# Output-gate loads of steps two to eight issued from GpSimd's queue instead of SyncE's

## The chip, the cores and the metric

The kernel runs on one core of one Trainium2 chip. The core has TensorE (PE), VectorE (DVE), ScalarE (ACT), GpSimd (POOL) and SyncE (SP), each with an instruction queue of its own that is worked through in order. The time is the device time of one execution in microseconds (us). Seven runs of the kernel before gave a median of 499.81 us, from 498.5 to 501.74.

## The reference

An mLSTM cell over 4 batches, 8 heads, 768 positions and a head width of 40 is followed by a feed-forward block with a leaky ReLU. Everything is float32. Cut to what matters:

```python
for t in range(S):
    m_new = max(f[t] + m, i[t]);  f_s = exp(f[t] + m - m_new);  i_s = exp(i[t] - m_new)
    C = f_s * C + i_s * outer(v[t], k[t]);   n = f_s * n + i_s * k[t]
    h = C @ q[t];   denom = max(abs(n . q[t]), 1)
    y[t] = sigmoid(o_gate[t]) * h / denom
x = y as (4*768, 8*40)
out = max(0.01 * (x @ w_in), x @ w_in) @ w_out      # 320 -> 2048 -> 320
```

The change touches only how `o_gate` comes into the on-chip memory. It is read at one place, the sigmoid in the last line of the loop.

## The kernel before, in words

**Tiling.** The 768 positions are cut into 12 chunks of 64, and a step is one chunk of two batches, so there are 24 steps, numbered 0 to 23. Steps 0 to 7, two groups of four, are "steps one to eight" of the change's title; the kernel's `s` counts from 0. A step on 128 partitions holds two batches of 64 positions and all 8 heads. A group of four steps makes 512 rows of `x`, on which the feed-forward block then runs; the first group uses plain matmuls (L863, L867, L970), later groups a form of Strassen's scheme with seven products (L919, L933, L1025).

**One step.** k and q come in (L500) and are turned on TensorE (L569, task T), copied out (L578, KC), and multiplied to scores (L610, SC). ACT makes the decay weights with eight exponentials (L551, E), DVE multiplies them into the scores (L618, P), TensorE applies them to the values (L692, PA), and the state C is read (L629, PC) and updated (L668, DC; L681/L679, CN; POOL's products L649, VU, and L656, CM). Then the denominator (L713 to L715, N), the output gate (ACT's tanh, L719, O, which reads the loaded `o_sb` tile; L726, G), the division (L731, XD), the turn of x (L740/L742, XT) and its copies (L756/L758, XC). A group's feed-forward products need the XC of its four steps. The tile `o_sb` has three buffers, so the load for step s waits until G of step s-3 has read the old one.

**Weights.** The weights arrive as 64-bit floats (L296/L301, L307, through three double buffers called raw) and are narrowed to 32 bits: one ACT instruction (L323, WA) and six DVE instructions (L341, L345, L349, L353, L355, L359, tasks WN) for each of the pieces 0 to 7 and each pair of later pieces. The first group's products (L863, task F j) need the narrowed piece j.

**What sets the order.** All work is put into a list of tasks, each with a due time, a cost per engine that may do it, and the tasks it needs. A greedy planner (class `Plan`, L19) places them one by one at the earliest time its costs allow, ties going to the earlier due time, and the instructions are then emitted in that order, engine by engine. Loads are tasks too, with SP as their engine; it also keeps one modelled wire on which all loads queue. So a changed cost or engine of one task can move every later task on every engine. Some transposes are preceded by fill matmuls whose results are not used (L559, `FILL`): seven before the turn of step 1's q and of step 1's x, nine before the turn of step 2's k, a few in step 4.

**Where the gate loads stand.** The load of an output gate is four DMA issues of 40 KB (L493), because heads and batches are interleaved over the partitions. They are planned in `plan_cell` (L763), in the loop at L771.

Of the kernel before, what the change touches and what calls it, by code (L numbers as in the profile page):

```python
# [18 lines left out]
class Plan:  # L19
# [9 lines left out]
    def add(self, name, key, ways, needs=(), takes=None, until=(), mode=None, wire=0.0):  # L29


        assert name not in self.tasks
        key += TUNE.get(name, 0.0) + (LATER.get(name[0], 0.0) if self.later else 0.0)
        self.tasks[name] = (key, ways, needs, takes, until, mode, wire)
# [105 lines left out]
def kernel(  # L140
# [26 lines left out]
    nc = tc.nc  # L167
# [7 lines left out]
    SG = 2 * PB  # L175
# [19 lines left out]
    def half(r):  # L195
        return slice(L * r, L * (r + 1))
# [170 lines left out]
    ACT, DVE, POOL, PE, SP = "ACT", "DVE", "POOL", "PE", "SP"  # L367
# [118 lines left out]
    def load(s, what, by=None):  # L486
        c, p = divmod(s, PB)
        d = st[s]
        if what == "o":
            d["o"] = wk.tile([P, H, D], F32, name="o_sb", bufs=NL)  # L490
            for r in range(2):
                for z in range(2):
                    (by or nc.sync).dma_start(  # L493
                        d["o"][half(r ^ z), ts(r, HH), :],
                        o_gate[2 * p + r, ts(z, HH), ts(c, L), :].rearrange("h p d -> p h d"),
                    )
            return
        dst, src = {"k": (d["kq"][0][:, :, :D], k), "q": (d["kq"][1][:, :, :D], q), "v": (d["va"][:, :, :D], v)}[what]
        for r in range(2):
            (by or nc.sync).dma_start(dst[half(r)], src[2 * p + r, :, ts(c, L), :].rearrange("h p d -> p h d"))  # L500
# [72 lines left out]
    def turned(s, i, copy):  # L573
        d = st[s]
        if "kqT" not in d:
            both = wk.tile([P, 2, PR, 2, P], F32, name="kqT")[:, 0].rearrange("p j r t -> p (j r t)")
            d["kqT"] = both.rearrange("p (i j r t) -> p i j r t", i=2, j=PR, r=2)
        copy(d["kqT"][:, i].rearrange("p j r t -> p j (r t)"), d.pop(("tp", i))[:])  # L578
# [118 lines left out]
    def valued(s, copy=None):  # L697
        d = st[s]
        pa = d.pop("pa")
        if copy:  # L700
            d["hn"] = wk.tile([P, H, D1], F32, name="hn")
        for r in range(2):
            to = d["hn"][:, ts(r, HH)]
            if copy:
                copy(to, pa[r][:])
            else:
                nc.vector.tensor_tensor(to, to, pa[r][:], op=ALU.add)
# [20 lines left out]
    def divide(s, by):  # L728
        d = st[s]
        x3 = d["x"][:].rearrange("p (h d) -> p h d", d=D)  # L730
        by.tensor_tensor(x3, x3, d["den"][:].unsqueeze(2).to_broadcast([P, H, D]), op=ALU.mult)  # L731
# [31 lines left out]
    def plan_cell(s):  # L763
# [7 lines left out]
        for what, old in (  # L771
            ("k", (("T", s - NL, 0), ("DC", s - NL))), ("q", (("T", s - NL, 1),)),
            ("v", (("VU", s - NL), ("PA", s - NL))), ("o", (("G", s - NL),)),
        ):
            if what == "q" and late_turn:
                continue
            ways = [(SP, 2.2 if what == "o" else 1.3, lambda what=what: load(s, what))]
            if (s, what) in ON_ACT:
                ways = [(ACT, 1.3, lambda what=what: load(s, what, nc.scalar))]
            add(("L", s, what), LOADS.get((s, what), at), ways, old, wire=1.4)  # L780
# [21 lines left out]
        for i in range(0 if late_turn else 2):  # L802
            add(("T", s, i), key[0], [(PE, 0.55, lambda i=i: turn(s, i))], [("L", s, "kq"[i]), ("SC", s - 2), ("PC", s - 2)], ("c", 1), [("KC", s, i)], mode=128)
            ways = [(ACT, 0.6, lambda i=i: turned(s, i, nc.scalar.copy))]
# [36 lines left out]
        if c > 0:  # L841
            ways = [(DVE, 0.62, lambda: valued(s))]
        else:
            ways = [(ACT, 0.8, lambda: valued(s, nc.scalar.copy)), (DVE, 0.62, lambda: valued(s, nc.vector.tensor_copy))]
# [4 lines left out]
        ways = [(POOL, 1.0, lambda: divide(s, nc.gpsimd))]  # L849
# [332 lines left out]
    for g in range(NG):  # L1182
        plan.later = g > 1
        for s in range(SG * g, SG * (g + 1)):
            plan_cell(s)
        plan.later = g > 0
        plan_first_ff() if g == 0 else plan_ff(g)
        if g == 0:
            for i in range(5):
                needs = [("IS", i - 1)] + list(done.values()) + ([("F", 0, j, h) for j in range(NP) for h in range(2)] if i > 2 else [])  # L1190
                plan.add(("IS", i), FF_1 - 20, [(DVE, 1.25, lambda i=i: in_sum(i))], needs)
                needs = [("WS", i - 1)] + list(done.values()) + ([("PT", n, m) for n in range(SG) for m in range(4)] if i > 2 else [])
                plan.add(("WS", i), FF_1 + PERIOD / 2 - 20, [(DVE, 1.55, lambda i=i: weight_sum(i))], needs)
# [36 lines left out]
```

## Time and profile before

| what | value |
|---|---|
| median of 7 runs | 499.81 us |
| the profiled execution's own time | 499.81 us |
| its span, first to last instruction | 498.0 us |
| busy: PE, DVE, ACT, POOL | 481.0, 375.7, 194.6, 90.4 us |
| granted TensorE clock, mean | 0.989 of full |
| DMA issues of the gate (L493) | 96, median 0.614 us to issue and 2.8 us from issue to landing |

The profile was taken in an execution that took 499.81 us, of which 1.81 us lie around the span. "Idle before" of an instruction is the time its engine stood idle ahead of it, with what ended it. SPq is the queue of DMA issues of SyncE. A window's PEclk is the mean TensorE clock granted in it, as a share of full speed.

### The profile page before, as it was taken

What the parts mean: (1) busy time and instruction counts of PE and PEld (TensorE: products, weight loads), DVE (VectorE), ACT (ScalarE), POOL (GpSimd) and SP (SyncE); (2) the same over time, 40 slices, a digit from 0 to 9 for tenths busy, and PEclk for the clock granted to TensorE, in tenths of its full rate; (3) what the DMA queues carried; (4) which work ended last, traced back from release to release, by engine and by line L of the source; (5) the groups of instructions that cost most, each with busy time, mean ns of one, the idle gap of its engine ahead of it and who ended that gap; (6) DMA issues with size and microseconds to landing.
All of it is one profiled execution on the core that took longest, in us unless ns stands there. A gap on an engine that the chain in (4) does not pass through costs nothing.

```text
span 498.0 us, 14150 instructions
## 1 busy us (share of the span) xinstructions
PE 481.0 (97%) x5622; PEld 406.5 (82%) x5622; DVE 375.7 (75%) x752; ACT 194.6 (39%) x583; POOL 90.4 (18%) x177
## 2 busy tenths in 40 slices
PE   7589899999999999999999999999999999999996
PEld 5457654677788899988899988899988899988996
DVE  4779599899999898887788688788788765445542
ACT  5452635533443552535532324641325630133200
POOL 2112001220140422403113303223202111000101
PEclk9889899999999999999999999999999999999999
DMA  6655777674564334554434453425343001100011
GB/s 126 146 122 111 214 222 165 176 132 93 117 152 78 84 75 113 119 108 97 88 65 121 80 112 72 86 37 142 75 94 71 3 1 28 26 2 0 1 28 26
DMA packets 119169, 44.95 MB, mean 90 GB/s; under 512 B 90624, under 2 KB 112448, under 8 KB 119104
## 3 DMA queue, kind: packets, MB, share of 16 engines
q1 hardware_dynamic: 117536, 43.50, 39.9%
q8 instruction: 44, 0.72, 0.6%
q10 hardware_dynamic: 1568, 0.56, 0.5%
q14 instruction: 21, 0.17, 0.1%
HBM read 40.01 MB, written 4.01 MB: 88 GB/s over the span
## 4 chain that ended last, share of the span: by engine, by line
PE 92%; SPq 3%; DMA 3%; issue 1%; ACT 0%; DVE 0%; ACTq 0%
PE po L1025 31%; PE phA L919 8%; PE po L970 7%; PE phC L919 7%; PE phB L919 7%; PE ph L863 6%; PE phB L933 4%; PE phD L919 3%; PE phD L933 3%; PE sc L610 3%; PE dC L668 2%; PE pa L692 2%; PE pc L629 2%; PE ph L867 2%; SPq L500 2%; PE tkq L569 1%
## 5 line engine op out<-in xcount | busy, mean ns | idle before, releaser
L1035 DVE TENSOR_TENSOR sums<-acts 128x1024 f32<-128x1024 f32 x50 | 62.2, 1263 | 17.8 <-PE po L1025 17.7
L1025 PE MATMUL po<-sums 128*128 128x160 f32 x480 | 69.3, 299 | 0.0
L1025 PEld LDWEIGHTS po<-sums 128*128 128x128 f32 x480 | 66.3, 190 | 0.2
L1032 ACT COPY s<-po 128x160 f32<-128x160 f32 x40 | 11.6, 291 | 91.2 <-PE po L1025 91.2
L1025 PE MATMUL po<-w_out,sums 128*128 128x160 f32 x320 | 47.1, 300 | 0.0
L731 POOL TENSOR_TENSOR x<-x,den 128x320 f32<-128x320 f32 x20 | 17.4, 868 | 163.2 <-DVE den L715 131.6
L1025 PE MATMUL po<-w_out,acts 128*128 128x160 f32 x320 | 45.8, 301 | 0.0
L551 ACT ACTIVATE w<-w,gT 128x64 f32<-128x64 f32 x160 | 40.2, 335 | 14.2 <-DVE w L542 10.6
L1025 PEld LDWEIGHTS po<-w_out,sums 128*128 128x128 f32 x320 | 44.4, 190 | 0.2
L1025 PEld LDWEIGHTS po<-w_out,acts 128*128 128x128 f32 x320 | 43.9, 190 | 0.5 <-issue 0.3
L945 ACT ACTIVATE acts<-phA 128x512 f32<-128x512 f32 x20 | 11.9, 596 | 71.5 <-PE phA L933 71.5
L970 PE MATMUL po<-w_out,acts 128*128 128x320 f32 x128 | 37.0, 437 | 0.0
L600 DVE STREAM_TRANSPOSE kqT<-q_all 128x512 f32<-128x512 f32 x32 | 34.8, 1102 | 0.0
L863 PE MATMUL ph<-xT,w_in 128*128 128x256 f32 (+1 forms) x96 | 31.4, 471 | 0.0
L970 PEld LDWEIGHTS po<-w_out,acts 128*128 128x128 f32 x128 | 23.4, 190 | 8.6
L649 POOL TENSOR_TENSOR vu<-va,gT 128x328 f32<-128x328 f32 x22 | 19.2, 874 | 57.2 <-DMA va<-in_v_dram 39.0
L1040 POOL TENSOR_TENSOR y<-s,s 128x160 f32<-128x160 f32 x10 | 12.3, 1226 | 89.9 <-ACT s L1032 89.9
L945 ACT ACTIVATE acts<-acts 128x512 f32<-128x512 f32 x40 | 24.6, 630 | 9.3 <-DVE acts L1095 9.3
L863 PEld LDWEIGHTS ph<-xT,w_in 128*128 128x128 f32 x96 | 17.9, 197 | 10.3 <-issue 7.8
L1095 DVE TENSOR_TENSOR acts<-sums,phD 128x512 f32<-128x512 f32 x20 | 13.6, 681 | 16.6 <-PE phC L933 16.6
L656 POOL TENSOR_TENSOR C<-C,gT 128x328 f32<-128x328 f32 x20 | 15.7, 786 | 52.6 <-DVE C L681 42.8
L758 ACT COPY xT<-xt 32x128 f32<-32x128 f32 x96 | 24.3, 253 | 0.9
(142 smaller groups left out, 1014.6 us busy)
## 6 DMA issues: line engine op xcount, KB each, us to landing
q_all<-in_q_dram SPq DMA_DIRECT2D x80, 80.0 KB, 2.3
raw<-in_moe_w_out_dram SPq DMA_DIRECT2D x8, 640.0 KB, 6.4
w<-a_dr SPq DMA_DIRECT2D x40, 128.0 KB, 3.0
q_all<-in_k_dram SPq DMA_DIRECT2D x64, 80.0 KB, 2.4
raw<-in_moe_w_in_dram SPq DMA_DIRECT2D x8, 512.0 KB, 4.7
k<-in_k_dram SPq DMA_DIRECT2D x48, 80.0 KB, 3.0
o_sb<-in_o_gate_dram SPq DMA_DIRECT2D x96, 40.0 KB, 2.8
va<-in_v_dram SPq DMA_DIRECT2D x46, 80.0 KB, 3.2
```

What stands on the lines that cost most here:

```text
L551: nc.scalar.activation(w[:, h, :], w[:, h, :] if c > 1 else st[s]["ab"][h], AF.Exp, bias=gT[:, c, 0, p, h : h + 1], scale=1.0,)
L600: nc.vector.transpose(lates[g, p][:, i, :, r, :].rearrange("p j (t x) -> p j x t", x=4), src)
L649: nc.gpsimd.tensor_tensor(d["vu"][:], d["va"][:], gT[:, c, 1, p].unsqueeze(2).to_broadcast([P, H, D1]), op=ALU.mult,)
L731: by.tensor_tensor(x3, x3, d["den"][:].unsqueeze(2).to_broadcast([P, H, D]), op=ALU.mult)
L758: nc.scalar.copy(xT[row : row + RH, KF, ts(b, P)].rearrange("p (r t) -> p r t", r=2), quarters[:RH, 1, at, :])
L863: nc.tensor.matmul(ph[:, cols], lhsT=w_full(kk, f), rhs=xTs[g][:, kk, cols], start=(kk == 0), stop=False)
L919: nc.tensor.matmul(po[g, j, bank][:, e], lhsT=a[:, 2 * j + e], rhs=x(), start=more != "add" and e == 0, stop=True, skip_group_check=True,)
L933: nc.tensor.matmul(po[g, j, bank][:, e], lhsT=w_rest(r, 2 * j + e), rhs=xTs[g][KR * r : KR * (r + 1), KF, ts(t, GH)], start=False, stop=Tr ...
L945: nc.scalar.activation(to, x, AF.Prelu, alpha=0.01)
L970: nc.tensor.matmul(po[n][:], lhsT=acts[:, FH * (f % 2) + f // 2, ts(n, P)], rhs=w_out[:, f, :], start=(f == 0), stop=(f == NF - 1),)
L1025: nc.tensor.matmul(po[g, n, bank][:], lhsT=a()[:, f, :], rhs=w()[:, f, :], start=not more and f == 0, stop=f == FH - 1, skip_group_check=True,
L1035: nc.vector.tensor_tensor(a_sums[slot], quarter(n, x), quarter(n, y), op=op)
```

## The change: what it does

For steps 1 to 7 the load of the output gate has POOL as its only engine, with a planned cost of 2.4 us in place of SP's 2.2 us, and its four DMAs are issued from GpSimd's queue. Step 0 and the steps from 8 on stay on SP. Nothing else is edited; the planner makes a new order from the new list.

```diff
             ways = [(SP, 2.2 if what == "o" else 1.3, lambda what=what: load(s, what))]
+            if what == "o" and 0 < s < 2 * SG:
+                ways = [(POOL, 2.4, lambda what=what: load(s, what, nc.gpsimd))]
             if (s, what) in ON_ACT:
                 ways = [(ACT, 1.3, lambda what=what: load(s, what, nc.scalar))]
             add(("L", s, what), LOADS.get((s, what), at), ways, old, wire=1.4)
```

`SG` is 4, so the condition holds for s from 1 to 7: 28 DMA issues in all.

## Prediction

> **What bounds the kernel now.** I read the page's busy row and its 40 slices, then the busy time by stretch, then the chain of waits and SP's and DVE's timelines of the first 60 us.
>
> ```profile
> PE 481.0 (97%) x5622; PEld 406.5 (82%) x5622; DVE 375.7 (75%) x752; ACT 194.6 (39%) x583; POOL 90.4 (18%) x177
> 0.00:20.00 20.00, 14.82 (x346) 11.15 (x346) 11.47 (x36) 10.48 (x35) 5.03 (x18) 1.00 0.62 133
> 20.00:40.00 20.00, 14.85 (x240) 10.32 (x237) 15.02 (x46) 10.46 (x36) 2.15 (x3) 0.83 0.58 124
> 40.00:60.00 20.00, 17.10 (x226) 12.39 (x224) 13.54 (x32) 8.97 (x25) 2.08 (x3) 0.91 0.67 165
> 60.00:80.00 20.00, 20.00 (x132) 10.69 (x132) 19.21 (x30) 9.08 (x25) 0.73 (x1) 1.00 0.79 197
> 140.00:180.00 40.00, 40.00 (x523) 34.18 (x522) 37.67 (x71) 17.78 (x47) 10.09 (x21) 1.00 0.50 106
> ```
>
> The columns after the length are the busy times of PE, PEld, DVE, ACT and POOL, then the TensorE clock. From 60 us on PE has no idle time until the last stretch: there only less PE work or nothing can help. The first 60 us hold 13.2 us of PE idle (5.2, 5.2 and 2.9) and clocks of 0.83 and 0.91. DVE is the second bound: 37.67 of 40 us from 140 to 180.
>
> The chain of waits in the opening (start, length), then who PE waited for there:
>
> ```profile
> 19.14 1.45 SPq L493
> 20.64 2.96 DMA o_sb<-in_o_gate_dram
> 24.08 1.73 ACT w L551 x8
> 26.05 3.14 PE xt L559 x7
> 47.98 1.35 SPq L500
> 50.12 2.90 DMA k<-in_k_dram
> ...
> PE tkq L569 <- DMA q_all<-in_q_dram: 3.9, 4, 2.3
> PE xt L559 <- ACT C L679: 3.4, 1, 3.4
> ```
>
> Two of the waits are SP's doing. The gate of step 1 lands at 23.6 us; ACT stands at its tanh, behind which are step 2's exponentials and the copy that frees a bank for XT of step 1, so PE waits 3.4 us. Then k and q of step 4 come late, behind 5.51 us of gate issues. In SP's timeline:
>
> ```profile
> 17.83 3.42 SPq L493 DMA_DIRECT2D o_sb<-in_o_gate_dram  x4
> 38.74 5.51 SPq L493 DMA_DIRECT2D o_sb<-in_o_gate_dram  x8
> 64.00 5.27 SPq L493 DMA_DIRECT2D o_sb<-in_o_gate_dram  x4
> ```
>
> **The change part by part.** The profiled execution took 499.81 us, span 498.0 plus 1.81 around it; that is also the median, so I count from 499.81.
>
> *SP loses 28 issues.* Before W4 is issued they are 3.42 + 5.51 = 8.9 us, so k and q of step 4, before at 47.31 to 50.72, go out some 9 us earlier and no longer hold PE at 51 to 53. DVE's 5.66 us of idle time before 57.77, a wait for W4, goes too. On its own this is worth up to the 3.4 + 2.7 us of PE waits plus the slow clock at 53 us.
>
> *POOL gains 28 issues.* Its order is now: gate 1, VU0, gate 2, CM2, VU1, gate 3, CM3, VU2, gate 4, CM4, VU3, gate 5, CM5, gate 6, VU4, and gate 7 before VU6. The trace has no POOL issue. Low bound: SP's 0.6 us; high bound: POOL's longest instruction, 1.45 us, say 1.5. It is done by POOL, where the 328-element products took 0.73 to 1.31 us, so I take 1.2: a gate costs 4.8 us (2.4 to 6.0). The waits for G(s-3) that are now on POOL hold only VU and CM, of which POOL had little to do: it was idle 20.3 us before VU4. So of these seven only gates 1 and 2 can hurt.
>
> *Gate 1 becomes the first thing ACT waits for.* In the new order ACT does O of step 1 ahead of the sixteen exponentials of steps 0 and 1, and DVE puts two of W0's narrowing instructions, which wait for ACT, ahead of P0. This is the new wait. POOL's last memset ends at 3.1; issuing ends at 7.9; landing is 2.8 - 0.6 = 2.2 later, 10.1. The exponentials then start at 10.5 and not 8.24. Queued behind them on ACT: CN0, step 0's q copy (14.8), WA0 (15.5). SC0 goes from 10.26 to 14.9. On DVE the two narrowing instructions end at 16.5, P0 at 17.3 (0.75), the rest of W0 (3.0) at 20.3, N, G and XD (1.6) at 22.0: XT of step 0 is at 22.0 and was at 17.31.
>
> *How much of that stays.* SC1 22.6, P1 23.9, PA1 24.8, its copy on ACT behind XC0 and E3 at 27.1, then N1, G1, XD1 at 28.8; on PE the nine and the seven fill matmuls put XT1 at 31 to 32, before 28.99. XC1 ends at 33.6. T, GT, SC and PC of steps 2 and 3 then run, and the first F starts at 34.6, before 33.79. From there DVE decides: from step 2's q copy, which ends at 33.3, to the end of W3's narrowing its new order has 18.5 us of instructions (0.5 to 0.85 each by the rows) and some ten hand-overs of 0.15 (PE's wait for one at 10.26 was 0.19): 53.3. So F of piece 3 starts at 53.3 (before 54.83) and the first F of the second half at 53.3 + 2.55 = 55.9. Before that was 58.12, with 0.7 us of slow clock in it. Result: -2.2 us.
>
> *POOL and DVE get in each other's way.* Before, one weight addition (L359) took 1.24 us beside POOL's VU and 0.82 alone:
>
> ```profile
> 18.98 1.24 DVE L359 TENSOR_TENSOR w_in<-w_in,wm 128x640 f32<-128x640 f32 x1
> 39.87 0.88 DVE L359 TENSOR_TENSOR w_in<-w_in,wm 128x640 f32<-128x640 f32 x1
> 51.28 0.83 DVE L359 TENSOR_TENSOR w_in<-w_in,wm 128x640 f32<-128x640 f32 x1
> ```
>
> About 12 POOL issues fall between 33 and 53 us, where DVE decides: 0 to 12 x 0.42 = 5.0 us. I take a third, since much of DVE's work there reads PSUM or is short: +1.7.
>
> The Trainium skill, "SBUF — State Buffer", section "SBUF: two separate sides", speaks against the change more strongly: a DMA issued from GpSimd has its descriptors written by GpSimd itself, which a VectorE copy can lock out, 0.62 us alone against 3.1 us beside one. By an estimate from that page a gate costs 2.5 us alone and 12.4 us under the weight narrowing, and the time would be 496 with the first and over 507 with the second; no row of before shows either.
>
> *The order after 60 us.* The planner's new list moves all later cells. I compared PE's order in PE work between dependent steps. (a) XT of step 15 now stands after the last product of group 2 with only one product (0.86 us) between it and the first one that needs its XC; in before a product of 2.2 us stood there as well. XC ends some 1.5 us after XT, plus a hand-over of 0.3: PE must wait 0.9 us. (b) Steps 8 and 9 come 13 and 12 us of PE work earlier, into the stretch from 139 to 171 us where DVE's timeline has one gap of 0.76 us. A late step costs DVE 4 x 1.10 + 0.70 + 0.73 + 0.56 + 0.56 + 0.55 + 0.6 + 0.5 = 8.6 us. If all of one step's work were extra there PE would wait about 5 us; but sums of weights (1.49 each) and a transpose leave the stretch. Bounds 0 and 5, I take 1.8, since the two orders differ there mostly by exchange. After step 19 the PE order is nearly the old one.
>
> Sum: -2.2 + 1.7 + 0.9 + 1.8 = +2.2, so 502.0 us.
>
> **The rivals.**
> *Faster: POOL issues as quickly as SP.* Place: ACT's first wait. At 0.6 us an issue, gate 1 lands at 7.7, before the 8.24 at which the exponentials start anyway; the opening gains 2.3 us more and nothing holds DVE: -4.5 in the opening, +0.9 for XT15, +0.3: 496.5. It decides once gate 1 lands by about 8.2. For it: POOL idle from 3.1 to 8.3, and a chain that names SP twice. Against: DVE's narrowing ahead of P0 stays.
> *They cancel.* -2.2, a little for DVE, 0.9 for XT15 and about 1 from the new order: 499.8. For it: PE runs gapless from 60 us, so each delay of others must first use up their lead.
> *Much slower: an issue holds POOL far longer.* If each took the 2.8 us from issue to landing, gate 1 would land near 16.5 and gate 2 near 28, and ACT has gate 2's tanh ahead of the copy of step 1's q, which was done by 17.7. The opening would lose 8 to 10 us: 510. Against: no POOL row over 1.45 us.
>
> **How the numbers follow.** Forecast 0.43 (its own range 500.5 to 505.0), faster 0.28, cancelled 0.15, much slower 0.14. Measurement tells about 0.3%, 1.5 us, from no change. So faster 0.28, same 0.15, slower 0.57. The range: 496.5 is the faster rival's centre with some tail left out below, 508 takes in the upper bounds of DVE's hold (+3.3 more) and of the new order (+3.2 more), together less likely than one; about 2 in 10 lie outside.
>
> **What would show it.** Right: ACT idle ahead of its tanh until about 10 us; XT0 near 22; no PE wait for q or k near 50; the first F of the second half near 56; a new PE wait of about 1 us near 285 us ahead of phB; PE waits for DVE between 140 and 180. Wrong: gate 1's tanh before 8.3 us; POOL issues near 0.6 us or above 2 us; PE gapless after 60 us, or a second slow-clock stretch before 20 us, where PE now stands idle from about 10 to 15.

## The result and the profile after

The changed kernel took 501.82 us (median of 29 runs, 500.81 to 504.46), the kernel before beside it 500.39 us (71 runs, 497.33 to 503.03). The ratio is 1.0039, with a 95% interval from 1.0027 to 1.0052: slower by 1.4 us in the medians and by 2.0 us by the ratio. The profiled execution took 500.81 us, with a span of 499.0 us, 1.0 us longer than that of before.

The page's busy row and the busy time by stretch of after; columns as in the prediction (length, then PE, PEld, DVE, ACT, POOL, the granted clock, DMA share, GB/s):

```profile
PE 483.9 (97%) x5622; PEld 406.9 (82%) x5622; DVE 376.5 (75%) x747; ACT 194.6 (39%) x588; POOL 108.7 (22%) x205
0.00:20.00 20.00, 13.87 (x232) 10.06 (x233) 10.50 (x33) 9.69 (x32) 9.49 (x26) 0.83 0.72 147
20.00:40.00 20.00, 17.32 (x358) 11.84 (x356) 13.55 (x39) 12.04 (x44) 7.95 (x12) 0.91 0.71 161
40.00:60.00 20.00, 18.73 (x236) 14.12 (x233) 18.92 (x41) 11.00 (x32) 6.67 (x10) 0.91 0.85 209
140.00:180.00 40.00, 38.87 (x513) 32.33 (x512) 33.78 (x76) 20.35 (x58) 7.12 (x16) 1.00 0.51 104
```

PE is less idle in the first 60 us (49.9 us busy, before 46.8), but part of that is the lower clock in the first 20. POOL has 18 us more. From 140 to 180 PE, gapless before, now waits.

How the gate loads are issued, by the summary of their line (shortest, median and longest issue in ns), and then what the view of DMA issues gives from issue to landing (median us last):

```profile
L493 SPq DMA_DIRECT2D o_sb<-in_o_gate_dram x68: 595/614/1799, 9.8 to 376.8; - x68
L493 POOL DMA_DIRECT2D o_sb<-in_o_gate_dram x28: 615/615/1187, 3.1 to 85.8; - x28
```

```profile
o_sb<-in_o_gate_dram SPq DMA_DIRECT2D x68, 40.0 KB, 2.6
o_sb<-in_o_gate_dram POOLq DMA_DIRECT2D x28, 40.0 KB, 3.9
```

An issue on POOL takes 0.615 us, as on SP, not the 1.2 us that I took; a gate some 2.5 and not 4.8.

The timelines of the engines at the places that the prediction named:

```profile
3.06 2.61 POOL L493 DMA_DIRECT2D o_sb<-in_o_gate_dram  x4
8.75 0.47 ACT L719 ACTIVATE o_sb<-o_sb 128x320 f32<-128x320 f32 x1 [1.82 <-DMA o_sb<-in_o_gate_dram]
9.13 3.36 ACT L551 ACTIVATE w<-ab,gT 128x64 f32<-128x64 f32 x16
...
13.41 1.13 PE L610 MATMUL sc<-kqT 40*64 40x64 f32 x32 [3.41 <-ACT kqT L578]
21.47 0.44 PE L740 MATMUL xt<-ident,x 128*128 128x128 f32 x2
...
154.11 0.44 PE L740 MATMUL xt<-ident,x 128*128 128x128 f32 x2 [1.13 <-POOL x L731]
285.64 1.13 PE L921 MATMUL phB<-xT,w_in 128*128 128x256 f32 x4 [0.18 <-ACT xT L756]
```

ACT does stand idle before gate 1's tanh, step 0's scores wait for its q copy, and XT0 comes at 21.47. The wait near 285 us is there, at a fifth of the forecast. A wait of 1.13 us at 154, XT of step 8, is new.

The chain of waits of the opening, which before went through the gate load of step 1:

```profile
22.56 3.45 DMA ig<-in_i_gate_dram
26.31 0.29 DVE m L387
...
31.37 0.40 DVE wm L341
31.96 1.67 PE xt L559 x7
...
34.54 0.70 DVE kqT L578
...
43.06 0.81 DVE w_in L349
...
47.60 3.10 PE ph L865 x8
```

It names no load of a gate of steps 1 to 7 any more (SP's four issues of step 0's gate are in it, from 9.76 us). From 26 to 32 us it is DVE's: gate scans, step 1's division, the start of piece 1's narrowing. Behind that PE and DVE take turns: PE's seven fill matmuls ahead of XT of step 1, DVE's copy of step 2's turned q (34.54), DVE's narrowing again (43.06), and PE's product of piece 2 at 47.60, which half clock (a granted clock of 0.50) stretches (3.10 us; the one of piece 0, at full clock, takes 1.92).

Stage by stage I use two marks. Group 1's first product (L919, in after L921) starts at 135.79 before and at 134.34 after: a lead of 1.45 us. From there to the end before needs 362.2 us and after 364.7: 1.46 more in group 1, 0.4 and 0.7 in the next two, nothing later. The other mark is the first product of piece 3 (L863, in after L865), at 54.83 before and 54.21 after.

### The profile page after: what moved, and what is told of

It is laid out like the page before. It is cut to its first block, busy times and chain, and to the rows that moved or that the text cites. A ratio compares the mean times of both kernels' runs of the same rounds, so it can differ in the third digit from the quotient of the medians.

```text
span 499.0 us, 14175 instructions
## 1 busy us (share of the span) xinstructions
PE 483.9 (97%) x5622; PEld 406.9 (82%) x5622; DVE 376.5 (75%) x747; ACT 194.6 (39%) x588; POOL 108.7 (22%) x205
## 4 chain that ended last, share of the span: by engine, by line
PE 91%; DMA 3%; SPq 2%; DVE 2%; issue 1%; POOL 0%; ACT 0%; DVEq 0%; POOLq 0%
PE po L1027 31%; PE phC L921 7%; PE phA L921 7%; PE po L972 7%; PE phB L921 7%; PE ph L865 6%; PE phB L935 4%; PE phD L921 3%; PE phD L935 3%; PE sc L610 3%; PE dC L668 2%; PE pa L692 2%; PE pc L629 2%; PE ph L869 2%; PE xt L740 1%; SPq L500 1%
## 5 line engine op out<-in xcount | busy, mean ns | idle before, releaser
L1037 DVE TENSOR_TENSOR sums<-acts 128x1024 f32<-128x1024 f32 x50 | 61.1, 1238 | 25.5 <-PE po L1027 24.5
L731 POOL TENSOR_TENSOR x<-x,den 128x320 f32<-128x320 f32 x20 | 18.6, 932 | 153.0 <-DVE den L715 112.3
L600 DVE STREAM_TRANSPOSE kqT<-q_all 128x512 f32<-128x512 f32 x32 | 35.4, 1108 | 0.0
L865 PE MATMUL ph<-xT,w_in 128*128 128x256 f32 (+1 forms) x96 | 31.7, 475 | 0.0
L1097 DVE TENSOR_TENSOR acts<-sums,phD 128x512 f32<-128x512 f32 x20 | 13.6, 682 | 22.3 <-PE phC L935 22.1
L656 POOL TENSOR_TENSOR C<-C,gT 128x328 f32<-128x328 f32 x20 | 19.4, 974 | 49.7 <-DMA fg<-in_f_gate_dram 21.8
L865 PEld LDWEIGHTS ph<-xT,w_in 128*128 128x128 f32 x96 | 18.1, 199 | 9.8 <-issue 7.0
L756 ACT COPY xT<-xt 128x128 f32<-128x128 f32 x48 | 12.7, 264 | 27.5 <-PE xt L742 26.9
```

What stands on the lines that cost most here:

```text
L600: nc.vector.transpose(lates[g, p][:, i, :, r, :].rearrange("p j (t x) -> p j x t", x=4), src)
L656: nc.gpsimd.tensor_tensor(C_t[(c + 1) % 2][:, two], C_t[c % 2][:, two], gL[:, c, two].unsqueeze(3).to_broadcast([P, 2, PR, D1]), op=ALU.mult,)
L865: nc.tensor.matmul(ph[:, cols], lhsT=w_full(kk, f), rhs=xTs[g][:, kk, cols], start=(kk == 0), stop=False)
L1037: nc.vector.tensor_tensor(a_sums[slot], quarter(n, x), quarter(n, y), op=op)
```

## The experiments

My theory after seeing the result: the queue by itself gains some 5 us, and the planner's new order, in the opening and after it, loses more than that. The rival: POOL's issues and the wait for gate 1 cost what is lost. "The list" below is the planner's list of tasks in order of emission, and `move(x, *y)` puts a task right behind the last of the tasks y.

**The queue and the order, each alone.** First the new order, all loads on SP:

```diff
-                ways = [(POOL, 2.4, lambda what=what: load(s, what, nc.gpsimd))]
+                ways = [(POOL, 2.4, lambda what=what: load(s, what))]
```

> The changed kernel's whole order, with the 28 gate loads issued from SP again. If the order is what costs and the queue is what helps (theory 1): SP now issues step 1's gate (2.7 us) ahead of everything else and carries the 8.9 us of gate issues ahead of W4 again, so it is the slowest of the four: 504 to 509. If issuing from POOL is what costs, by its later landing (3.9 us against 2.8) or by holding DVE (theory 2): at or below the changed kernel's 501.8.

It took 507.95 us, 1.0156 of before (1.0122 to 1.019). Then the reverse: before, with the planner still told that SP issues, so that no task changes its place, and the issue itself on POOL:

```diff
-            ways = [(SP, 2.2 if what == "o" else 1.3, lambda what=what: load(s, what))]
+            ways = [(SP, 2.2 if what == "o" else 1.3, lambda what=what: load(s, what, nc.gpsimd if what == "o" and 0 < s < 2 * SG else None))]
```

> The old list and the old order on PE, DVE and ACT; only the queue of the 28 loads is POOL's. Theory 1: both PE waits that SP caused go (3.4 us ahead of XT of step 1, 2.7 us for q and k of step 4), nothing new stands in front of ACT's first exponentials, and nothing moves after 60 us: 2 to 5 us faster than before, 495.5 to 498.5. Theory 2: no faster than before, 500.5 to 502.

It took 495.58 us, 0.9906 of before (0.9878 to 0.9934). So the queue gains 4.8 us in the old order (500.34 to 495.58) and 6.1 in the new (507.95 to 501.82); the new order costs 6.2 us on POOL and 7.6 on SP. Both parts of the theory hold. In the trace group 1 starts at 130.58, 5.2 us earlier than before, and from there to the end takes the 362.2 us of before.

**The new order cut in two.** New order and POOL up to the planner's task I4 of group 1, old order behind it; and the reverse, old opening with loads on SP, new order behind it:

```diff
+        old = plan.order()          # then the tasks ("L", s, "o") are given POOL as in the change
+        new = plan.order()
+        opening = {x[2] for x in old[:cut]}          # cut: where ("I4", 1, 0) stands
-        for at, _, name, emit in plan.order():
+        for at, _, name, emit in [x for x in new if x[2] in opening] + [x for x in old if x[2] not in opening]:
```

> The changed kernel's order and POOL loads up to the first product of group 1 (I4), the old order from there on. Theory 1: keeps the opening's lead of 1.4 us and loses none of it later: 498.5 to 499.5. Theory 3, that the profile pair flatters the opening and its gain is not there in most executions: 500.4 to 501.5.

> The old opening with SP loads, the changed kernel's order from the first product of group 1 on. Theory 1: the 1.13 us wait ahead of XT of step 8, 0.2 us ahead of group 3 and some 1 us of more frequent switches on PE, with no lead to pay for them: 502 to 503.5. Theory 3: the later order costs nothing in the median, 500 to 501.

The first took 498.9 us, 0.9992 of before (0.997 to 1.0014); from the seam on it needs the time of before. Against after's 501.82 that is 2.9 us for the later part of the order; against the old order on POOL, 495.58, it is 3.3 us for the order of the opening. The second was a miss: 511.64 us, 1.0232 (1.0199 to 1.0265), forecast 502 to 503.5. The seam itself made a wait that neither kernel has; who PE waited for after 60 us in it:

```profile
PE sc L610 <- DVE kqT L600: 6.7, 1, 6.7
PE xt L740 <- POOL x L731: 1.4, 1, 1.4
PE phB L919 <- ACT xT L756: 0.2, 1, 0.2
```

6.7 us are a wait for DVE's turn of k and q (L600), late only where the two orders meet. The run doesn't price the later order, but it shows again waits of 1.4 and 0.2 us at the two places of the new order.

**Is it the wait for gate 1?** After, with ACT's tanh of step 1 put behind the exponentials of steps 0 and 1:

```diff
+        move(("O", 1), ("E", 1))
```

> The changed kernel, with ACT's tanh of step 1 moved behind the exponentials of steps 0 and 1. If that wait is what makes the new opening late (the prediction's step), the exponentials start at 8.2 us as before instead of 9.13, and all that follows on ACT, from step 0's q copy on, comes 0.9 us earlier: first product of group 1 at about 133.4 in place of 134.34, time 0.5 to 1 us under the changed kernel's. If the wait is only a small part, because the q copy stands behind the exponentials in any case: no more than that; if it were the main part: 3 to 4 us.

It took 501.29 us, 1.0033 (1.0014 to 1.0053). Step 0's scores start at 12.28 instead of 13.41, but XT0 at 21.52, and group 1 at 134.43. The time is 0.5 us under after's, inside the noise (after's ratio is 1.0027 to 1.0052). The wait is real and costs nothing that lasts.

**Is it step 0's chain?** Two runs. In the first its q copy goes from ACT to DVE, and P0 ahead of W0's narrowing:

```diff
+        move(("KC", 0, 1), ("KC", 0, 0), ("T", 0, 1))[1] = lambda: turned(0, 1, nc.vector.tensor_copy)
+        move(("P", 0), ("SC", 0), ("E", 0))
```

> The changed kernel, with the copy of step 0's turned q given back to DVE, right behind k's, and P of step 0 ahead of the two narrowing instructions; gate 1's tanh stays first on ACT. If ACT's queue ahead of the q copy is what makes the opening late: PE's wait of 3.41 us ahead of the scores of step 0 shrinks to under 0.7, the scores start near 10.7, the turn of step 0's x near 18.5 to 19.5 in place of 21.47, and the first product of group 1 at 131 to 132.5: 498 to 499.5 us. If DVE's order further down is what decides (it does the weights' narrowing as one chain): XT of step 0 comes earlier but group 1 starts at 133.5 or later, and the time stays above 500.5.

502.25 us, 1.0025 (1.0003 to 1.0046): a miss for the theory that forecast a gain. PE's wait ahead of the first scores falls from 3.41 to 0.78 us and XT0 stays at 21.39. Group 1 starts at 136.50 in its trace, 2.2 us later than in after; that trace has the long stretch of half clock, from 25.1 to 35.3 us, whose price is shown under "Is it the clock?". The second brings the whole chain forward:

```diff
+        for name, *behind in (
+            [("HA", 0), ("KC", 1, 0)], [("N", 0), ("HA", 0)], [("G", 0), ("N", 0)], [("XD", 0), ("G", 0)],
+            [("XT", 0), ("XD", 0), ("T", 1, 1)],
+        ):
+            move(name, *behind)
+        for i in range(6):
+            move(("WN", 0, i), ("WN", 0, i - 1) if i else ("XD", 0))
```

> Change against the kernel after: step 0's chain is put together as the old order has it. As in q_copy_dve its q copy is on DVE and P0 ahead of W0's narrowing; in addition HA0 goes behind the k copy of step 1 on ACT, N0, G0 and XD0 ahead of all six of W0's narrowing instructions on DVE, and XT of step 0 on PE right behind step 1's q turn, ahead of MK2 and SPR2. Theory A (it is W0's narrowing ahead of step 0's chain that costs the opening): XT of step 0 at 18.8 to 20 us instead of 21.47, the first product of group 1 at 132 to 133.4 instead of 134.34, time 499 to 500.5. Theory B (the place of no single cell chain decides; over the opening PE is idle nearly as long as in the old order with loads on POOL, 7.7 against 7.0 us, and the same instructions take 124.5 instead of 121.2 us, since more of them fall into half clock): XT0 2 us earlier, but the first product of group 1 within 0.7 us of 134.34 unless the half clock moves, and time 501 to 502.5.

XT0 goes from 21.47 to 18.02, the place that it has in the old order (18.23 with POOL), and group 1 still starts at 134.09; 501.2 us, 1.0032 (1.0014 to 1.0051). Its trace has more half clock from 20 to 40 us than after's (24.0 to 30.9 us), so the 0.25 us are not exact; but the median of 12 runs, 0.6 us under after's and inside the noise, leaves step 0's chain little to be worth.

**Is it step 1's chain?**

```diff
+        for name in ("HA", "N", "G", "XD", "XT"):
+            move((name, 1), *((("PA", 1),) if name == "HA" else ((before, 1),)))
+            before = name
```

> Change against the kernel after: step 1's value chain is put right behind PA1 on every engine: on PE, XT of step 1 goes ahead of the nine fill matmuls before T of step 2, ahead of GT2 and ahead of DC2; on DVE, N1, G1 and XD1 go ahead of GD3; on ACT, the copy HA1 goes ahead of CN1. Everything else is as in after. Theory A (the new order of PE and DVE in the opening decides): XT of step 1 at 28 to 30 us instead of 33.47, the first first-layer product of group 1 at 131.5 to 133 instead of 134.34, time 498.5 to 500.5. Theory B (the clock's slow stretches or DVE's whole chain of weight narrowing decide, XT1 is not on the path): XT1 earlier by 3 us or more, but the first F and the first product of group 1 where they were within 0.5 us, time 501 to 502.5.

A miss for both: XT1 comes at 30.48, 3 us earlier, and the time rises to 504.9 us, 1.011 (1.0078 to 1.0141). What was moved ahead made the second of the gate scans late (30.11 us, in after 27.53), and DVE then waits more often for PE (2.06 us for the turned gates of L427, with the first instruction for piece 1 at 31.82); its trace also has a stretch of half clock, from 37.7 to 41.1 us, that after's doesn't have. So the run mixes two causes. In it PE waits 2.12 us for DVE's w_in at 57.76, and group 1 starts at 139.53.

**Is it the clock?** "Half clock" is time in which the granted TensorE clock is 0.50. After has half clock from 12.4 to 19.2, 26.1 to 29.5 and 46.6 to 50.0 us (13.6 us), the old order on POOL only from 23.2 to 26.6. PE stands idle just ahead of the first stretch, so I gave it ten fill matmuls there:

```diff
-FILL = {("T", 1, 1): 7, ("XT", 1): 7, ("T", 2, 0): 9, ("T", 4, 0): 3, ("T", 4, 1): 2}
+FILL = {("T", 0, 1): 10, ("T", 1, 1): 7, ("XT", 1): 7, ("T", 2, 0): 9, ("T", 4, 0): 3, ("T", 4, 1): 2}
```

> Change against the kernel after: ten more fill matmuls ahead of step 0's turn of q, in the stretch from 10 to 13.4 us in which PE waits for ACT's copy. The order is otherwise that of after. Theory A (the half clock from 12.4 to 19.2 us follows from PE's idle time there, and costs part of the 3.8 us by which the opening of after is behind the old order with loads on POOL): no half clock before 22 us, the seven fill matmuls before T of step 1 take 1.5 to 1.8 us instead of 2.96, XT of step 0 at 20 to 21, group 1's first product 0.7 to 2 us earlier, time 499.5 to 501. Theory B (DVE's order sets XT0 and what follows): the half clock gone or moved, XT0 still at 21 to 21.8, group 1 within 0.5 us of 134.34, time 501 to 502.5.

503.34 us, 1.0087 (1.0053 to 1.0121). The test was badly built: the fills stand ahead of the q turn whose copy PE then waits for, so the first scores came 3.1 us later, at 16.52, and nothing on the clock's share follows from the time. The half clock wasn't avoided either, though the row of that stretch says 1.00. PE's timeline of this run, and of the old order on POOL, where the same matmul runs at full clock:

```profile
11.36 4.04 PE L559 MATMUL tkq<-cmask_b,ident_b 128*128 128x512 bf16 x10
15.24 0.60 PE L569 MATMUL tkq<-ident,q_all 128*128 128x128 f32 x4
```

```profile
12.87 1.67 PE L559 MATMUL tkq<-cmask_b,ident_b 128*128 128x512 bf16 x7
```

0.40 us for one against 0.24.

The price of the half clock can be read from a run made for another question. xt8_later, which comes next, has after's order throughout the opening, but in its trace the half clock lasts from 25.4 to 35.6 us, 10.2 us in place of after's 3.4. Up to there the two traces are alike (XT0 at 21.33 and 21.47). The stretch from 20 to 40 us, for which after's line is shown above:

```profile
20.00:40.00 20.00, 17.41 (x333) 11.67 (x332) 11.05 (x36) 11.27 (x42) 7.07 (x12) 0.74 0.73 164
```

DVE does 2.5 us less there, since PE's turn of step 2's q comes later. DVE's copy of it starts at 37.13 for 34.54, the first product of piece 3 at 56.79 for 54.21, and group 1 at 136.92 for 134.34. So with one and the same order 6.8 us more of half clock made the opening 2.6 us later, and a difference of that size between two single traces tells nothing of the order. (open_new, with the same opening and 3.4 us of half clock at that place, has piece 3 at 54.79.)

**The later wait.** XT of step 8 moved behind the next first-layer product:

```diff
+        move(("XT", 8), ("I5", 1, 2))
```

> The changed kernel, with the turn of step 8's x two products (1.73 us) later on PE. If the 1.13 us wait ahead of it is a real loss: it goes, and all later groups start 1.0 to 1.1 us earlier, group 2 at 209.1 in place of 210.16. If DVE's backlog is what sets the pace there, the wait comes back at another place within group 1 and group 2 starts as before, at 210.2.

501.62 us, 1.0029 (1.001 to 1.0049). The 1.13 us are gone, but two new waits of 0.16 and 0.17 us stand near 156 and 177 us, and group 1 lasts 75.36 us for 75.82: a gain of 0.5 where the wait was 1.1. (Group 2 starts at 212.28, not at 210.2 or before, because of the late opening just described.)

**SP freed, or POOL used?** The old order again, the 28 issues on ACT's queue (`nc.scalar` for `nc.gpsimd` in the second diff):

> Change against the kernel before: the old order, with the 28 gate loads of steps 1 to 7 issued from ACT's queue, not from SP's and not from POOL's. It tells 'SP freed' from 'an idle queue used'. Theory A (what gains is an idle engine to issue from): 28 issues at 0.6 us are 17 us in ACT's in-order stream, about 10 of them before 60 us, ahead of exponentials and q copies; SP is freed as with POOL, so the 5 us gained are partly or wholly given back: 497 to 502. Theory B (all of the gain is SP's being freed, whoever issues): 495 to 496.5, as with POOL.

500.67 us, 1.0029 (1.0004 to 1.0054). An issue takes 0.627 us there too, but ACT's own work stands behind it. From ACT's timeline:

```profile
15.79 5.34 ACTq L493 DMA_DIRECT2D o_sb<-in_o_gate_dram  x3
21.17 1.07 ACT L578 COPY kqT<-tkq 128x512 f32<-128x512 f32 x2 [4.98 <-DMA o_sb<-in_o_gate_dram]
```

Step 1's q copy comes after 5 us in which ACT does no other work, and PE waits 3.9 us for it. So freeing SP isn't enough: the gain needs a queue with nothing urgent behind the issues, and that was POOL.

**A version that beats both.** The old order with step 0's gate on POOL as well (`s < 2 * SG` alone as the condition):

> The old order, with the gate of step 0 on POOL as well, eight gates in all. In the run with seven the longest PE wait left is 2.79 us at 17.3 for step 1's q, which SP issues behind step 0's gate (2.7 us). If the queue is what counts: that wait shrinks by up to 2.7 us and the time falls 1 to 2.5 us below the run with seven, 493 to 494.5. If the wait is covered by others, or POOL's first products are held up behind the gate: 495 to 496.5.

494.4 us (493.94 to 494.82), 0.9885 of before (0.9861 to 0.9908). In the old order on POOL, PE still waited 2.8 us for step 1's q, which SP issues behind the 2.6 us of step 0's gate; with step 0's gate on POOL that wait is gone. In its place PE waits 0.9 and 0.3 us for k and q of step 0, and 10 us of the first 20 are at half clock; group 1 starts where it did (130.65). Against seven gates on POOL the gain is 1.2 us in the medians of 5 and 6 runs, and the intervals of the two ratios overlap: that both versions beat before and after is shown, that the eighth gate adds to it isn't.

## Why the opening of the new order is later

The comparison that answers it is after against the old order on POOL, which have the same loads on the same queues and differ in order; the medians give 3.3 us for the opening's order (above). Up to the first product of piece 3 (54.21 and 50.31 us) DVE has narrowed the same four weight pieces. DVE's busy time (third number behind the length) by stretch in after, then in the old order on POOL:

```profile
20.00:40.00 20.00, 17.32 (x358) 11.84 (x356) 13.55 (x39) 12.04 (x44) 7.95 (x12) 0.91 0.71 161
40.00:54.20 14.20, 12.94 (x209) 10.01 (x206) 13.52 (x32) 5.64 (x16) 5.66 (x9) 0.88 0.82 201
```

```profile
20.00:40.00 20.00, 18.01 (x303) 12.52 (x292) 19.20 (x49) 11.62 (x41) 7.90 (x13) 0.91 0.74 173
40.00:50.30 10.30, 8.84 (x194) 6.72 (x194) 9.82 (x27) 5.24 (x17) 3.95 (x7) 1.00 0.87 227
```

From 40 us on DVE is full in both (all but 0.7 and 0.5 us), and in eleven of the fourteen traces, both of these among them, the first product of piece 3 starts 0.14 or 0.15 us behind the end of DVE's last instruction for the piece. So its work decides when piece 3 can start; but between 20 and 40 it stands idle for 6.4 us in after and 0.8 in the other. The difference, 5.6, covers the 3.9 us by which piece 3 is late; after's DVE has 1.5 us less to do by then (37.6 us for 39.1), in part because ACT copies `hn` there. What DVE waits for is in its timeline, and what it could have done is in ACT's. After:

```profile
22.78 0.75 DVE L618 TENSOR_TENSOR w<-w,sc 128x256 f32<-128x256 f32 x2 [2.01 <-PE sc L610]
25.71 0.28 DVE L380 TENSOR_TENSOR_SCAN F<-fg,zeros 32x64 f32<-32x64 f32 x1 [2.17 <-DMA fg<-in_f_gate_dram]
31.28 0.49 DVE L341 TENSOR_SCALAR wm<-w_in 128x640 f32<-128x640 f32 x1
34.54 0.69 DVE L578 COPY kqT<-tkq 128x512 f32<-128x512 f32 x1 [1.62 <-PE tkq L569]
...
24.65 1.75 ACT L551 ACTIVATE w<-ab,gT 128x64 f32<-128x64 f32 x8
27.41 0.77 ACT L323 ACTIVATE w_in<-raw 128x640 f32<-128x640 f32 x1
```

The old order on POOL:

```profile
22.66 0.49 DVE L341 TENSOR_SCALAR wm<-w_in 128x640 f32<-128x640 f32 x1
23.18 0.49 DVE L345 TENSOR_SCALAR wm<-wm 128x640 uint32<-128x640 uint32 x1
...
21.23 0.79 ACT L323 ACTIVATE w_in<-raw 128x640 f32<-128x640 f32 x1 [0.87 <-DMA raw<-in_moe_w_in_dram]
```

In the old order ACT narrows its part of piece 1 as the data land, at 21.23, and DVE starts its six instructions at 22.66, in time that is otherwise waiting. The new order has the ACT part at 27.41, behind the exponentials of steps 2 and 3, with no wait of its own, and DVE starts piece 1 at 31.28, behind gate scans that wait for their DMA. Nothing later makes up for it.

The half clock has a part in it too. Of DVE's idle time in after, the 1.62 us at 34.54 are a wait for a turn that PE makes behind nine fill matmuls; these took 3.49 us, at half clock, and in the old order 2.11 at full clock. And it isn't an accident of one trace: over its executions after has a median of 14.5 us of half clock (30 executions), open_new 13.9 (12), and the old order on POOL 5.9 (6). How much of the opening's 3.3 us is the narrowing's place, and how much the half clock that the order brings with it, stays open.

The mark carries over all runs: in twelve of the fourteen kernels group 1 starts 80.05 to 80.27 us after the first product of piece 3; in before and in xt1_first it is 80.96 and 81.77, with a half-clock stretch just behind the mark. So whatever leaves piece 3 where it is (gate 1, step 0's chain) leaves the time where it is. That piece 1's late narrowing is the main part is argued from these two traces and not shown; a version of after with that part alone put back wasn't run.

## Why the prediction was right, and by which errors

The forecast of 502.0 us, slower, came out at 501.82, but not by its own terms. That the two agree to 0.2 us is luck: it counted from 499.81, and the 71 runs of before have a median of 500.39; its change of +2.2 stands against +1.4 in the medians (+2.0 by the ratio). In the profiled pair the change is +1.0 us, and against the forecast sum:

| term | forecast | measured |
|---|---|---|
| opening | -2.2 | -1.45 |
| POOL's issues hold DVE | +1.7 | about 0 (inside the opening) |
| XT of step 15 ahead of phB (one of the seven products) | +0.9 | +0.18 |
| order after 60 us, the rest | +1.8 | +2.3 |
| sum | +2.2 | +1.0 |

- **SP loses 28 issues: right.** The first issue of step 4's q is at 39.27 and was at 47.31 before; PE has no wait for k or q near 50 us. Alone the queue gains 4.8 us, inside the bound given (the waits of 3.4 and 2.7 us).
- **"I take 1.2: a gate costs 4.8 us": mis-sized by two.** The low bound was true: 0.615 us. Landing took longer than I had it, 3.9 us from issue for 2.8, so that gate 1's tanh ran at 8.75: the forecast said 10.1, the rival 7.7. The high bound and the words "no POOL row over 1.45 us" were a misreading, without effect: before has POOL rows of 1.79 us (L731 at 162.10, L649 at 277.31).
- **"This is the new wait": there, and of no price.** SC0 at 13.41 (forecast 14.9), XT0 at 21.47 (22.0), XT1 at 33.47 (31 to 32). gate1_behind and xt0_first took the wait and the late XT0 away, and the times stayed within 0.6 us of after's. A chain that I followed link by link through four engines was not the one that ended last.
- **"From there DVE decides": right, and it is the step that carries the opening.** Forecast 53.3 us for piece 3, measured 54.21; first product of the second half 55.9, measured 56.74. Two errors partly cancel in it: step 2's q copy ended at 35.23 and not at 33.3, and from there to the end of piece 3's narrowing (54.06) DVE took 18.8 us and not 20.0. The cause of DVE's lateness wasn't in the prediction: it counted instructions from 33.3 us on, but the loss is DVE's idle time from 20 to 35.
- **"POOL and DVE get in each other's way": not by DMA issues.** From DVE's timeline of after, and POOL's beside it:

```profile
37.82 1.21 DVE L355 SCALAR_TENSOR_TENSOR wm<-raw,wm 128x640 f32<-128x640 uint32 x1
43.05 0.82 DVE L349 SCALAR_TENSOR_TENSOR w_in<-raw,wm 128x640 uint32<-128x640 uint32 x1
...
37.62 0.73 POOL L649 TENSOR_TENSOR vu<-va,gT 128x328 f32<-128x328 f32 x1
42.90 2.46 POOL L493 DMA_DIRECT2D o_sb<-in_o_gate_dram  x4 [4.55 <-DVE x L726]
```

  L349 during an issue takes the 0.82 us that it takes alone (L353, just behind it, 0.57 for 0.49); L355 beside POOL's product takes 1.21 for 0.83. I had carried a figure from POOL's elementwise work over to its issues. The Trainium skill, "SBUF — State Buffer", section "SBUF: two separate sides", states that a DMA issued from GpSimd which takes some 620 ns alone takes some 3100 ns beside a VectorE copy. The prediction took these for times of an issue; the page gives them for the DMA. No lengthening of that size is seen here in either: the 28 issues, several of them beside weight narrowing, have a median of 0.615 us and a maximum of 1.187, and from issue to landing the same loads took 3.9 us from POOL's queue in after, 3.8 from ACT's in oldorder_act and 3.0 from SP's in before. Whether a VectorE instruction of the kind that the page means ran beside them isn't shown.
- **The order after 60 us: right in size and sign.** 2.5 us for 2.7 with XT15. The largest piece isn't a wait for DVE, as I had it, but 1.13 us for POOL's division of step 8. Of the rest, the 0.4 us of group 2 hold no wait above 0.1 us, and of the 0.7 us of group 3 only 0.18 are one (the one near 285 us). The cause of what is left was not tested; that +2.3 came so near to +1.8 is in part luck.
- **The faster rival: its condition came true and its time didn't.** "POOL issues as quickly as SP" was the case, and in the old order it gave 495.58 us, near its 496.5. In after the new opening took 3.8 us of it (134.34 for 130.58) and the later order 2.5.
- **The clock** was named only among the signs of error. The stretch before 20 us came, and what it cost isn't shown. The one behind it has a price: 2.6 us of the opening when it lasted 10.2 us and not 3.4 (xt8_later against after). The sum has no term for it.

## What to carry to other kernels

In a kernel whose order a planner makes, giving a task another engine is two edits, another queue and another order; run each alone before judging either. Here the queue was worth 1% and the order lost more than that, and keeping the old order on the new queue beats both kernels. To find what ends an opening, take a mark that all versions share and ask which engine has no idle time ahead of it; then look for that engine's idle time earlier, not for the longest new wait. And compare medians of many executions where the clock can move a single trace by more than the change is worth.

## What the hardware showed that was not expected

- An issue of this 40 KB load takes the same time from three queues, 0.614 us on SP, 0.615 on POOL, 0.627 on ACT (medians). From issue to landing the loads of steps 1 to 7 took 3.9 us from POOL's queue (after), 3.8 from ACT's (oldorder_act) and 3.0 from SP's (before); SP's 2.6 in after are mostly loads of later steps, when the DMA share is 0.4 to 0.5 and not 0.7 to 0.85, so they don't compare.
- In after POOL's DMA issues left DVE's narrowing instructions within 0.1 us of their lone durations (in the old order on POOL one L353 took 0.69 us for 0.49); POOL's elementwise products lengthened some of them by half, and in the old order on POOL one to double (L353, 0.98 us for 0.49).
- The granted clock of a row can miss half clock: in fill_q0 the row says 1.00, and a matmul that takes 0.24 us took 0.40 for 4 us.
- How long the half clock lasts differs from execution to execution of one kernel: 3 to 22 us over the 80 executions of before beside the experiments (twice one minus the mean clock, by the span). Their times rise by 0.15 us for each microsecond of it, loosely (correlation 0.47); over the 30 executions of after there is no such relation (0.02). How much of it there is doesn't by itself tell the time.
- In the fourteen traces each recorded stretch of half clock lasts 3.4 us or a small multiple of it (6.8, 10.2, 13.7), but for the last one, behind which the profile ends.
